# Exponentials of score tiles on VectorE: one pair with two private buffers, or two pairs that borrow their intermediates, in a new order

## The chip, the cores and the metric

The kernel runs on one core of one Trainium2 chip. The metric is the time of one execution in device microseconds; the kernel before took 1028.12 us (median of three runs, 1028.08 to 1029.24). TensorE does the matrix products, ScalarE (ACT in the profile) the exponentials and other activations, VectorE (DVE) most of the elementwise work, GpSimd (POOL) some small statistics and products, and SyncE (SP) issues most transfers.

## The reference

Two rounds of an attention layer and a mixer, over one sequence of 2048 positions with 448 channels. Attention has 16 heads of 28 channels. All weights are bfloat16.

```python
def _A_ref(x, wqkv, wo):                      # attention
    q, k, v = ...                             # x @ wqkv, split in 16 heads
    scores = jnp.einsum("bhqd,bhkd->bhqk", q, k) * (Dh ** -0.5)
    p = _softmax(scores, axis=-1)
    o = jnp.einsum("bhqk,bhkd->bhqd", p, v)
    return (...)(o, 0, 2, 1, 3).reshape(B, S, D) @ wo

def _B_ref(x, w1, w2, w3, w4):                # mixer
    h = _gelu(_layernorm(x, axis=-1) @ w1)
    ...                                       # four channel groups, shifted by -1, +1, -2, +2 positions
    hs = jnp.concatenate([g0, g1, g2, g3], axis=-1) @ w2
    x1 = x + hs
    h2 = _gelu(_layernorm(x1, axis=-1) @ w3) @ w4
    return x1 + h2

x = x + _A_ref(_layernorm(x, axis=-1), A_wqkv, A_wo)
x = x + _B_ref(_layernorm(x, axis=-1), B_w1, B_w2, B_w3, B_w4)
...                                           # the same two lines once more
```

What weighs most is the softmax: 2 layers x 16 heads x 2048 x 2048 exponentials, which is 2048 tiles of 128 x 512 scores.

## The kernel before

**A planner writes the order.** The program has no loops on the chip. While it is built, a planner (`Sched.run`) runs many small tasks, written as generators. Each yields operations with a planned duration and the tiles that they read and write, or asks for a resource (`acq`, `try`) or a signal. The planner hands the operations to five queues (TensorE, ScalarE, VectorE, GpSimd, SyncE), one by one, by its own planned clock and by priorities, and `Plan` then adds the semaphore waits. On the chip each engine works through its queue strictly in that order. So a number in a table of priorities or rates can move every instruction behind it.

**Scores.** Keys lie on the partitions. A score tile is 128 keys x 512 queries of one head. Four heads go together, so a block of 128 keys has four tiles. The queries are cut into chunks, the keys into ranges, and a *segment* is a chunk, a range and a group of four heads; there are 68 segments. `t_scores` takes the tiles in a fixed stream and puts them in turn into PSUM banks 0 to 2 (up to three tiles) and 3 to 5 (two tiles, now and then three). `t_exp` lets ScalarE turn each such unit into bfloat16 probabilities in `PT` (L1786, an instruction of 128x1024 or 128x1536). `t_pv` multiplies them with the values (L832), and sums in bank 7 over a segment. At the end of a segment VectorE copies bank 7 out (L1870, L1872).

**Tiles on VectorE.** Some tiles do not go to ScalarE. `t_scores` looks some key blocks ahead (`ahead_of`), and takes a tile there either into bank 2 in place of a unit's third tile (rates `R_RATE`, 6 to 8 blocks ahead) or into a free bank 5 or 6 (rates `D_RATE`, 5 to 7 blocks ahead). `d_first` (L1600) scales the tile out of PSUM into a 16-bit buffer `y`, and `d_chain` makes the exponential from the bits: a shift (L1627), a square (L1632), two multiply-and-adds (L1634, L1636), a product (L1638), a sum back into `y` (L1640), and per tile a last shift into a probability tile (L1646). Two tiles share a chain where two come soon enough after one another (a *pair*, 1024 wide); otherwise the chain is closed with one (512 wide). The width of the chain's operations is that of the pair, so a pair pays each of six instructions once.

**Buffers of a chain.** `y` and the first intermediate `q` are the two halves of `yd` (4 KB per partition, one pair at a time), or, in two stretches of the program in which some tiles of `vaug` are idle, four such tiles. The second intermediate `z` is a float buffer: one of the three `fb`, which the mixers' tanh steps (L2066 to L2069) and the softmax's normalization (L1893, L1897) use too, or in those stretches two tiles of `vaug`.

**The mixers** and projections run in between, on TensorE (L841), with their evacuations on VectorE and some elementwise steps on VectorE or GpSimd (table `XPAR`). Where TensorE would be idle in the plan, filler matmuls (L2299) are put in.

Of the kernel before, what the change touches and what calls it, by code (L numbers as in the profile page):

```python
# [552 lines left out]
R_RATE = {(0,): 0, (1,): 0.006, (2,): 0.016, (3,): 0.04, (4,): 0.006, (5,): 0.238, (6,): 0.059, (7,): 0.106, (8,): 0.06, (9,): 0.048, (10,): 0.024, (11,): 0.15, (12,): 0.066, (13,): 0.022, (14,): 0.018, (15,): 0.192, (16,): 0.233, (17,): 0.06, (18,): 0.115, (19,): 0, (20,): 0.093, (21,): 0.233, (22,): 0.355, (23,): 0.29, (24,): 0, (25,): 0.289, (26,): 0, (27,): 0.207, (28,): 0.183, (29,): 0.243, (30,): 0.071, (31,): 0.163, (32,): 0.241, (33,): 0.078}  # L553
# [22 lines left out]
XPAR = {'l0': 10, 'l1': 13, 'l2': 17, 'x0': 17, ('mg', 0, 0): 1, ('mg', 0, 1): 1, ('mg', 0, 2): 0, ('mg', 0, 3): 1, ('mg', 0, 4): 0, ('mg', 1, 0): 2, ('mg', 1, 1): 1, ('mg', 1, 2): 0, ('mg', 1, 3): 0, ('mg', 1, 4): 1, ('tw', 0, 0): 0, ('tw', 0, 3): 0, ('tw', 0, 7): 0, ('tw', 0, 11): 1, ('tw', 0, 13): 0, ('tw', 1, 0): 0, ('tw', 1, 3): 0, ('tw', 1, 7): 0, ('tw', 1, 11): 0, ('tw', 1, 13): 0, ('ek', 0, 0): 2, ('eo', 0, 0): 0, ('ek', 0, 1): 1, ('eo', 0, 1): 2, ('ek', 0, 2): 1, ('eo', 0, 2): 2, ('ek', 0, 3): 0, ('eo', 0, 3): 1, ('ek', 0, 4): 1, ('eo', 0, 4): 2, ('eq', 0, 0): 2, ('eq', 0, 1): 1, ('eq', 0, 2): 1, ('eq', 0, 3): 2, ('ez', 0, 0): 1, ('ez', 0, 3): 0, ('ez', 0, 7): 1, ('ez', 0, 11): 1, ('ez', 0, 13): 0, ('ez', 0, 4): 0, ('ez', 0, 8): 2, ('ez', 0, 12): 2, ('ez', 0, 14): 1, ('ex', 0, 0): 0, ('ex', 0, 1): 1, ('ex', 0, 2): 2, ('ex', 0, 3): 0, ('ex', 0, 4): 2, ('ex', 0, 5): 0, ('ex', 0, 6): 1, ('ex', 0, 7): 1, ('ex', 0, 8): 1, ('ex', 0, 9): 2, ('ex', 0, 10): 1, ('ex', 0, 11): 1, ('ex', 0, 12): 1, ('ex', 0, 13): 1, ('ex', 0, 14): 1, ('ex', 0, 15): 1, ('ek', 1, 0): 0, ('eo', 1, 0): 2, ('ek', 1, 1): 2, ('eo', 1, 1): 0, ('ek', 1, 2): 2, ('eo', 1, 2): 1, ('ek', 1, 3): 1, ('eo', 1, 3): 0, ('ek', 1, 4): 2, ('eo', 1, 4): 1, ('eq', 1, 0): 2, ('eq', 1, 1): 2, ('eq', 1, 2): 2, ('eq', 1, 3): 0, ('ez', 1, 0): 2, ('ez', 1, 3): 2, ('ez', 1, 7): 1, ('ez', 1, 11): 2, ('ez', 1, 13): 2, ('ez', 1, 4): 2, ('ez', 1, 8): 0, ('ez', 1, 12): 1, ('ez', 1, 14): 1, ('ex', 1, 0): 0, ('ex', 1, 1): 1, ('ex', 1, 2): 0, ('ex', 1, 3): 2, ('ex', 1, 4): 2, ('ex', 1, 5): 2, ('ex', 1, 6): 0, ('ex', 1, 7): 2, ('ex', 1, 8): 2, ('ex', 1, 9): 2, ('ex', 1, 10): 0, ('ex', 1, 11): 2, ('ex', 1, 12): 2, ('ex', 1, 13): 2, ('ex', 1, 14): 1, ('ex', 1, 15): 0, ('dt', 0): 0.742, ('dt', 1): 0.628, ('dt', 2): 0.754, ('dt', 3): 0.95, ('dt', 4): 0.834, ('dt', 5): 0.726, ('dt', 6): 0.327, ('dt', 7): 0.769, ('dt', 8): 0.514, ('dt', 9): 0.919, ('dt', 10): 0.95, ('dt', 11): 0.935, ('dt', 12): 0.755, ('dt', 13): 0.521, ('dt', 14): 0.877, ('dt', 15): 0.62, ('dt', 16): 0.663, ('dp', 0): 2.391, ('dp', 1): 2.567, ('dp', 2): 3.153, ('dp', 3): 2.433, ('dp', 4): 3.2, ('dp', 5): 1.698, ('dp', 6): 2.869, ('dp', 7): 1.898, ('dp', 8): 2.378, ('dp', 9): 2.988, ('dp', 10): 3.2, ('dp', 11): 3.081, ('dp', 12): 3.111, ('dp', 13): 3.2, ('dp', 14): 3.192, ('dp', 15): 3.2, ('dp', 16): 2.069, ('wt', 0): 0.173, ('wt', 1): 0.214, ('wt', 2): 0.438, ('wt', 3): 0.198, ('wt', 4): 0.329, ('wt', 5): 0.329, ('wt', 6): 0.17, ('wt', 7): 0.332, ('wt', 8): 0.414, ('wt', 9): 0.157, ('wt', 10): 0.38, ('wt', 11): 0.078, ('wt', 12): 0.009, ('wt', 13): 0.041, ('wt', 14): 0.163, ('wt', 15): 0.173, ('wt', 16): 0.372, ('ft', 0): 0.152, ('ft', 1): 0.146, ('ft', 2): 0.121, ('ft', 3): 0.157, ('ft', 4): 0.109, ('ft', 5): 0.073, ('ft', 6): 0.146, ('ft', 7): 0.029, ('ft', 8): 0.164, ('ft', 9): 0.024, ('ft', 10): 0.115, ('ft', 11): 0.041, ('ft', 12): 0.072, ('ft', 13): 0.183, ('ft', 14): 0.2, ('ft', 15): 0.146, ('ft', 16): 0.146, ('rp', 0): 1.476, ('rp', 1): 1.076, ('rp', 2): 0.876, ('rp', 3): 0.794, ('rp', 4): 0.794, ('rp', 5): 0.715, ('rp', 6): 0.645, ('rp', 7): 1.183, ('rp', 8): 0.857, ('rp', 9): 0.794, ('rp', 10): 0.842, ('rp', 11): 0.725, ('rp', 12): 0.707, ('rp', 13): 1.158, ('rp', 14): 0.794, ('rp', 15): 0.794, ('rp', 16): 0.621, ('pw', 0): 2, ('pw', 1): 2, ('pw', 2): 2, ('pw', 3): 2, ('pw', 4): 2, ('pw', 5): 4, ('pw', 6): 2, ('pw', 7): 3, ('pw', 8): 2, ('pw', 9): 4, ('pw', 10): 3, ('pw', 11): 1, ('pw', 12): 2, ('pw', 13): 3, ('pw', 14): 4, ('pw', 15): 2, ('pw', 16): 3}  # L576
# [25 lines left out]
def build_kernel(nc, A_x, A_wqkv, A_wo, B_x, B_w1, B_w2, B_w3, B_w4, out, n_layers=2):  # L602
# [79 lines left out]
    with st:  # L682
# [855 lines left out]
        def xtra(kind):  # L1538
            for ph, base in ((0, 16), (1, 9)):
                if ("xopen", ph) in SC.events and ("xshut", ph) not in SC.events:  # L1540
                    return {"y": ["ypv%d" % base], "f": ["fv%d" % (base + 4)], "pd": ["pv%d" % (base + 6)]}[kind]
            return []

        def t_extra(ph, base):
# [4 lines left out]
            for r in ("ypv%d" % base, "fv%d" % (base + 4), "pv%d" % (base + 6)):  # L1549
                yield ("acq", [r])  # L1550
# [14 lines left out]
        def ybuf(r):  # L1565
            if r[2] == "v":
                v, k = vbuf(r)
                w = vaug[:, int(r[3:]) + 2:int(r[3:]) + 4, :].rearrange("p a b -> p (a b)")
                return v, k, w, [("vaug", int(r[3:]) + 2), ("vaug", int(r[3:]) + 3)]
            return yd[:, 0, :], [("yd", 0)], yd[:, 1, :], [("yd", 1)]  # L1570
# [7 lines left out]
        def pbuf(r):  # L1578
            return ("vaug" if r[1] == "v" else "pd", int(r[2:]))

        PDS = ["pd%d" % i for i in range(NPD)]
        YS = ["yp0"]
        half = [None]

        def pair_of(ys, u):
# [817 lines left out]
```

## Time and profile before

| | |
|---|---|
| median of three runs | 1028.12 us (1028.08 to 1029.24) |
| the profiled execution | 1027.51 us, of it 1025.8 us span |
| TensorE busy | 973.4 us (95%), fillers included |
| ScalarE busy | 977.2 us (95%) |
| VectorE busy | 815.3 us (79%) |
| GpSimd busy | 194.8 us (19%) |
| granted TensorE clock | 1.00 |

Busy is the time in which an engine works on at least one instruction; instructions of one engine can overlap at their ends, so a group's mean duration times its count can be more than its busy time. The span leaves 1.7 us around it.

### The profile page before, as it was taken

Reading aid. Unit: us, or ns where it says so; the run is one execution under the profiler, and the core shown is the slowest. Engines: PE = TensorE matmul, PEld = TensorE weight load, DVE = VectorE, ACT = ScalarE, POOL = GpSimd, SP = SyncE. Lnnn points to the kernel's source line nnn. Section 1 sums busy time; section 2 is a strip of 40 time slices with the busy share of each in tenths; the row PEclk is TensorE's granted clock in tenths of the full one; section 3 lists DMA queues with packets and bytes.
Section 4 is the critical chain, followed back from the end, with each engine's and each line's share of the span. In section 5 each row is a group of like instructions: output and inputs, shape, how many; then the busy total and the mean of one; then the engine's idle time right before and its main releaser. Section 6 shows DMA issues by size and latency. Waiting matters only on the chain.

```text
span 1025.8 us, 36020 instructions
## 1 busy us (share of the span) xinstructions
PE 973.4 (95%) x16095; PEld 403.7 (39%) x16098; DVE 815.3 (79%) x1826; ACT 977.2 (95%) x900; POOL 194.8 (19%) x327
## 2 busy tenths in 40 slices
PE   8999999999999999999999999999999999999998
PEld 4333433433343334443434333333333333444465
DVE  8879999898757767887689779999898888787751
ACT  6899999999999999999999999999999999999933
POOL 4004012212222112220211000001431110431120
PEclk9999999999999999999999999999999999999999
DMA  4535324411113123220123124333311110231000
GB/s 126 130 73 167 64 54 106 146 31 46 25 22 96 24 67 69 52 44 14 43 61 82 42 71 132 110 75 101 84 28 34 41 45 13 55 61 18 12 21 25
DMA packets 98827, 64.41 MB, mean 63 GB/s; under 512 B 70832, under 2 KB 87552, under 8 KB 98672
## 3 DMA queue, kind: packets, MB, share of 16 engines
q1 hardware_dynamic: 94176, 53.11, 21.0%
q0 software_dynamic: 3376, 8.09, 2.9%
q8 instruction: 126, 2.06, 0.9%
q10 hardware_dynamic: 1120, 0.92, 0.3%
q14 instruction: 29, 0.24, 0.1%
HBM read 28.16 MB, written 16.76 MB: 44 GB/s over the span
## 4 chain that ended last, share of the span: by engine, by line
ACT 68%; PE 25%; DVE 6%; issue 1%; DMA 0%; ACTq 0%; DVEq 0%
ACT PT L1786 62%; PE ps L841 14%; PE ps L1488 6%; PE ps L832 4%; ACT h2T L2252 3%; ACT fb L2068 1%; ACT L1786 1%; DVE yd L1600 0%; DMA PT<-in_A_wqkv_dram 0%; ACT hT L2050 0%; PE ps L2299 0%; ACT L2252 0%; DVE vaug L1634 0%; DVE fb L1638 0%; ACT vaug L2252 0%
## 5 line engine op out<-in xcount | busy, mean ns | idle before, releaser
L1786 ACT ACTIVATE PT<-ps 128x1024 bf16<-128x1024 f32 (+1 forms) x793 | 882.0, 1304 | 6.0 <-PE ps L1488 4.9
L1488 PE MATMUL ps<-qT,kT 32*128 32x512 bf16 (+1 forms) x2560 | 310.1, 340 | 28.0 <-ACT PT L1786 20.7
L832 PE MATMUL ps<-PT,vaug 128*32 128x512 bf16 (+1 forms) x2411 | 244.1, 341 | 0.0
L1488 PEld LDWEIGHTS ps<-qT,kT 32*128 32x128 bf16 x2560 | 79.8, 91 | 298.8 <-ACT PT L1786 271.8
L841 PE MATMUL ps<-xT,w 128*32 128x512 bf16 (+4 forms) x2304 | 149.4, 336 | 0.0
L2299 PE MATMUL ps<-ident 128*32 128x256 bf16 x2900 | 132.6, 279 | 2.3 <-POOL ident L931 1.5
L832 PEld LDWEIGHTS ps<-PT,vaug 128*32 128x32 bf16 x2411 | 72.6, 94 | 90.8 <-issue 76.9
L841 PE MATMUL ps<-w,h2T 128*32 128x448 bf16 x1288 | 90.2, 355 | 3.7 <-ACT h2T L2252 3.7
L2299 PEld LDWEIGHTS ps<-ident 128*32 128x32 bf16 x2900 | 80.9, 98 | 28.8 <-issue 12.6
L1600 DVE TENSOR_SCALAR yd<-ps 128x512 int16<-128x512 f32 x84 | 57.7, 687 | 32.5 <-PE ps L1488 31.2
L841 PEld LDWEIGHTS ps<-xT,w 128*32 128x32 bf16 (+1 forms) x2304 | 61.1, 95 | 42.5 <-issue 22.5
L1897 POOL TENSOR_TENSOR otn<-ub,fb 128x512 bf16<-128x512 f32 (+1 forms) x27 | 32.5, 1205 | 220.2 <-DMA fb<-rscr 211.6
L2228 DVE CAST h2T<-ps 128x384 bf16<-128x384 f32 (+1 forms) x84 | 52.2, 621 | 20.4 <-PE ps L841 19.3
L841 PEld LDWEIGHTS ps<-w,h2T 128*32 128x32 bf16 x1288 | 33.9, 96 | 32.5 <-issue 12.8
L841 PE MATMUL ps<-kT,w 128*32 128x512 bf16 (+4 forms) x576 | 45.3, 350 | 0.9 <-DVE h2T L2228 0.5
L841 PE MATMUL ps<-xT,wq_pad 128*32 128x512 bf16 x512 | 45.0, 382 | 0.9 <-DVE kT L1227 0.8
L832 PE MATMUL ps<-PD,vaug 128*32 128x512 bf16 (+1 forms) x131 | 41.3, 347 | 0.8 <-DVE PD L1646 0.8
L841 PE MATMUL ps<-xT,wk_pad 128*32 128x512 bf16 (+2 forms) x512 | 38.9, 362 | 2.0 <-DVE kT L1227 1.4
L841 PE MATMUL ps<-wo_pad,otn 128*32 128x448 bf16 x512 | 37.4, 355 | 1.5 <-DVE x_res L1952 1.5
L841 PE MATMUL ps<-w,hT 112*32 112x448 bf16 x512 | 34.9, 355 | 4.1 <-ACT hT L2050 2.2
L2141 POOL TENSOR_SCALAR mst<-mv 128x1 f32<-128x1 f32 x32 | 8.8, 285 | 154.9 <-DVE mv L1052 154.9
L841 PE MATMUL ps<-wv,xT 128*32 128x448 bf16 x464 | 36.1, 356 | 1.2 <-DVE vaug L1334 0.4
(234 smaller groups left out, 1290.8 us busy)
## 6 DMA issues: line engine op xcount, KB each, us to landing
uscr<-ub SPq DMA_DIRECT2D x28, 256.0 KB
ub<-uscr SPq DMA_DIRECT2D x28, 256.0 KB, 2.8
fb<-rscr SPq DMA_DIRECT2D x96, 64.0 KB, 2.1
xnd<-xn SPq DMA_DIRECT2D x28, 128.0 KB, 2.5
x_res<-in_A_x_dram POOLq DMA_DIRECT2D x16, 224.0 KB, 2.7
xd<-x_res SPq DMA_DIRECT2D x16, 224.0 KB, 3.5
x_res<-xd SPq DMA_DIRECT2D x16, 224.0 KB, 4.2
out_dram<-obf SPq DMA_DIRECT2D x16, 112.0 KB
```

Of the source, the lines that this page charges most:

```text
L832: return lambda e: e.matmul(out=out, lhsT=lhsT, rhs=rhs, start=start, stop=stop, **kw)
L841: r.append(e.matmul(out=out[c:c + w, :], lhsT=lhsT[:, c:c + w], rhs=rhs, start=start, stop=stop, tile_position=(0, c)))
L1488: yield op("pe", (0.005 + NW * 0.00042) / nc_, lambda e, i=i, kc=kc, j=j, g=g, a=a, NW=NW, bank=bank: e.matmul(out=ps[:, bank, i * NW:(i + ...
L1600: yield op("dve", c_ps(512), lambda e: e.tensor_scalar(out=y.bitcast(I16)[:, 512 * h:512 * h + 512], in0=ps[:, bi(bank), :], scalar1=SCALE ...
L1786: yield op("act", 0.0635 + n * w * 0.000833, lambda e, bk=bk, s0=s0, n=n, w=w: e.activation(out=PT[:, s0:s0 + n, 0:w], in_=ps[:, bk[0]:bk[ ...
L1897: yield both(("eo", L, ch), 0.2 + NW * 0.00225, 0.07 + NW * 0.00104, lambda e: e.tensor_tensor(out=otn[:, g, 0:NW], in0=u, in1=rb[:, 0:NW] ...
L2068: yield op("act", c_act(NW), lambda e: e.activation(out=f, in_=f, func=ACT.Tanh, scale=8.0 * GK * (2.0 / math.pi) ** 0.5), reads=[fk], wri ...
L2141: yield op("pool", 0.2, lambda e: e.tensor_scalar(out=mst[:, t, V3E:V3E + 1], in0=mv[:, t, 1:2], scalar1=EPS, scalar2=None, op0=ALU.add), ...
L2228: ev = op("dve", c_ps(m * NW), lambda e, hr=hr, pv=pv: e.tensor_copy(out=hr, in_=pv), reads=[("ps", bi(b))], writes=hk, touch=[b])
L2252: yield op("act", c_act(len(fr_) * NW), lambda e, v=v: e.activation(out=v, in_=v, func=ACT.Gelu_apprx_tanh), reads=allk, writes=allk, tab= ...
L2299: return [e.matmul(out=ps[32 * c:32 * c + 32, bi(b), 0:256].rearrange("p (a n) -> p a n", n=128), lhsT=xn[:, 0, D:D + 32] if live else ide ...
```

## The change

The change has two parts. In the buffers, `y` and the first intermediate are parted: `yd` now holds two `y` of 2 KB each (`yp0`, `yp1`), so that two pairs can be under way, and the first intermediate becomes a second float buffer, which the chain asks for before its first shift and gives back at its end. The list of float buffers of the two idle stretches grows by the tiles that the first intermediate had there. In the order, five tables of the planner have other numbers: the rates at which tiles are taken (`R_RATE`, `D_RATE`), priorities (`RANK`), lead times (`Q_LEAD`) and `XPAR` (which engine takes some elementwise steps, thresholds and chain priorities).

```diff
-R_RATE = {(0,): 0, (1,): 0.006, (2,): 0.016, (3,): 0.04, (4,): 0.006, (5,): 0.238, (6,): 0.059, (7,): 0.106, (8,): 0.06, ...}
+R_RATE = {(0,): 0, (1,): 0.006, (2,): 0.016, (3,): 0.04, (4,): 0.006, (5,): 0.238, (6,): 0.037, (7,): 0, (8,): 0.169, ...}
...
@@ xtra
-                    return {"y": ["ypv%d" % base], "f": ["fv%d" % (base + 4)], "pd": ["pv%d" % (base + 6)]}[kind]
+                    return {"y": ["ypv%d" % base], "f": ["fv%d" % (base + 2), "fv%d" % (base + 4)], "pd": ["pv%d" % (base + 6)]}[kind]
@@ t_extra
-            for r in ("ypv%d" % base, "fv%d" % (base + 4), "pv%d" % (base + 6)):
+            for r in ("ypv%d" % base, "fv%d" % (base + 2), "fv%d" % (base + 4), "pv%d" % (base + 6)):
@@ ybuf
             if r[2] == "v":
-                v, k = vbuf(r)
-                w = vaug[:, int(r[3:]) + 2:int(r[3:]) + 4, :].rearrange("p a b -> p (a b)")
-                return v, k, w, [("vaug", int(r[3:]) + 2), ("vaug", int(r[3:]) + 3)]
-            return yd[:, 0, :], [("yd", 0)], yd[:, 1, :], [("yd", 1)]
+                return vbuf(r)
+            return yd[:, int(r[2:]), :], [("yd", int(r[2:]))]
@@
-        YS = ["yp0"]
+        YS = ["yp0", "yp1"]
@@ d_first
-            y, yk, _, _ = ybuf(pr["y"])
+            y, yk = ybuf(pr["y"])
@@ d_chain
-            y, yk, q, qk = ybuf(pr["y"])
+            y, yk = ybuf(pr["y"])
+            fq = yield ("acq", xtra("f") + FB, yk)
+            q_, qk = fbuf(fq)
+            q = q_.bitcast(BF16)
...
             yield ("rel", fr)
+            yield ("rel", fq)
```

More of the change, by code (lines that the diff above doesn't have):

```diff
@@ L552 @@
 DSEG = 1
-R_RATE = {(0,): 0, (1,): 0.006, (2,): 0.016, (3,): 0.04, (4,): 0.006, (5,): 0.238, (6,): 0.059, (7,): 0.106, (8,): 0.06, (9,): 0.048, (10,): 0.024, (11,): 0.15, (12,): 0.066, (13,): 0.022, (14,): 0.018, (15,): 0.192, (16,): 0.233, (17,): 0.06, (18,): 0.115, (19,): 0, (20,): 0.093, (21,): 0.233, (22,): 0.355, (23,): 0.29, (24,): 0, (25,): 0.289, (26,): 0, (27,): 0.207, (28,): 0.183, (29,): 0.243, (30,): 0.071, (31,): 0.163, (32,): 0.241, (33,): 0.078}
+R_RATE = {(0,): 0, (1,): 0.006, (2,): 0.016, (3,): 0.04, (4,): 0.006, (5,): 0.238, (6,): 0.037, (7,): 0, (8,): 0.169, (9,): 0.238, (10,): 0.048, (11,): 0.076, (12,): 0.066, (13,): 0.022, (14,): 0, (15,): 0.192, (16,): 0.156, (17,): 0.242, (18,): 0.053, (19,): 0.098, (20,): 0, (21,): 0.159, (22,): 0.357, (23,): 0.386, (24,): 0, (25,): 0.289, (26,): 0, (27,): 0.207, (28,): 0.255, (29,): 0.266, (30,): 0.098, (31,): 0, (32,): 0.241, (33,): 0.065}
 RLO = 6
@@ new lines @@
+Q_LEAD = {(0, 1): 7, (0, 2): 95, (0, 3): 64, (1, 0): 30, (1, 1): 99, (1, 2): 9, (1, 3): 66}
+D_RATE = {(0,): 0, (1,): 0, (2,): 0, (3,): 0.517, (4,): 0.133, (5,): 0.289, (6,): 0.447, (7,): 0.362, (8,): 0.092, (9,): 0.3, (10,): 0.129, (11,): 0.512, (12,): 0.005, (13,): 0.687, (14,): 0, (15,): 0.045, (16,): 0, (17,): 0.061, (18,): 0, (19,): 0.166, (20,): 0.403, (21,): 0, (22,): 0.477, (23,): 0, (24,): 0.39, (25,): 0, (26,): 0.293, (27,): 0.385, (28,): 0.064, (29,): 0.61, (30,): 0, (31,): 0.226, (32,): 0.513, (33,): 0.301}
```

6 lines of the change are left out of this document (2 added, 4 removed).

## The prediction

> **What bounds the kernel now.** I read the page first, its engine totals and the chain that ended last, then ScalarE's busy time by windows.
>
> ```profile
> PE 973.4 (95%) x16095; PEld 403.7 (39%) x16098; DVE 815.3 (79%) x1826; ACT 977.2 (95%) x900; POOL 194.8 (19%) x327
> ACT 68%; PE 25%; DVE 6%; issue 1%; DMA 0%; ACTq 0%; DVEq 0%
> ```
> ```profile
> core 0: us, PE busy (x) PEld busy (x) DVE busy (x) ACT busy (x) POOL busy (x), PEclk, DMA share, GB/s
> 0.00:25.00 25.00, 20.59 (x360) 10.88 (x361) 21.26 (x77) 17.05 (x24) 9.73 (x23) 1.00 0.42 129
> 25.00:100.00 75.00, 72.18 (x994) 24.82 (x1000) 61.31 (x147) 69.69 (x65) 14.72 (x21) 1.00 0.49 122
> sum 800.00, PE 761.23 PEld 304.00 DVE 657.32 ACT 798.14 POOL 146.56; mean PE 95.15 PEld 38.00 DVE 82.17 ACT 99.77 POOL 18.32
> ```
>
> Columns are a window's length and each engine's busy time with its count; the last row sums the eight windows of 100 us from 100 to 900. There ScalarE works 798.14 of 800 us, VectorE 657, 82%. TensorE's 95% is no bound of the same kind: the planner fills its gaps with filler matmuls. ScalarE has a hole of 8.0 us in the first 25 us, 5.3 in the next 75, almost none to 900, and after its last exponential it is not the bound: TensorE works off the last mixers. So a microsecond of exponentials taken off ScalarE is a microsecond of span, as long as TensorE and VectorE bring score tiles in time.
>
> What does an exponential cost? Instructions overlap at their ends, so I go by start to start.
>
> ```profile
> L1786 ACT ACTIVATE PT<-ps 128x1536 bf16<-128x1536 f32 x337 | 515.0, 1553 | 5.5 <-PE ps L1488 4.6
> L1786 ACT ACTIVATE PT<-ps 128x1024 bf16<-128x1024 f32 x456 | 483.6, 1120 | 0.5 <-PE ps L1488 0.3
> ```
> ```profile
> 361.08 57.80 ACT PT L1786 x52
> 952.27 1.34 ACT PT L1786
> 953.92 0.91 ACT PT L1786
> 972.16 1.28 ACT L2224
> ```
>
> The first fence groups instructions by form (count, busy, mean ns); the second is the chain in order of time (start, length, what). A step with three tiles takes 1.34, one with two 0.91 us, together 2.25 for five tiles; 52 unbroken steps give 57.80/26 = 2.22 per two. A tile is worth 0.45 us of ScalarE. The last row is the table load behind the last exponential, at 972.16: from there to the end of the span it is 53.6 us.
>
> **What the change removes.** The order that the changed program is built in has 334 instructions of 1536 and 453 of 1024: three fewer of each, 15 tiles, which VectorE takes (140 first operations L1600, 125 before). ScalarE's other work keeps its number of table loads (16), and one evacuation and one longer GELU swap. Removed: 3 x 2.25 = **6.8 us**.
>
> **What it adds on VectorE.** The words of the change promise pairs, but the order shows the reverse: chains of two fall from 43 to 31, chains of one rise from 39 to 78 (2 x 43 + 39 = 125; 2 x 31 + 78 = 140). Durations first, a chain of one that runs alone, then one whose operations alternate with others' (start, length):
>
> ```profile
> 660.42 0.29 DVE L1627 TENSOR_SCALAR vaug<-vaug 128x512 uint16<-128x512 uint16 x1
> 660.74 0.43 DVE L1632 TENSOR_TENSOR vaug<-vaug 128x512 bf16<-128x512 int16 x1
> 661.20 0.29 DVE L1634 TENSOR_SCALAR vaug<-vaug 128x512 bf16<-128x512 int16 x1
> 661.41 0.29 DVE L1636 TENSOR_SCALAR vaug<-vaug 128x512 bf16<-128x512 bf16 x1
> 661.73 0.43 DVE L1638 TENSOR_TENSOR vaug<-vaug 128x512 bf16<-128x512 bf16 x1
> 662.19 0.43 DVE L1640 TENSOR_TENSOR vaug<-vaug 128x512 int16<-128x512 int16 x1
> ...
> 674.93 0.28 DVE L1627 TENSOR_SCALAR vaug<-vaug 128x512 uint16<-128x512 uint16 x1
> 675.13 0.41 DVE L1640 TENSOR_TENSOR yd<-yd,fb 128x512 int16<-128x512 int16 x1
> 675.47 0.41 DVE L1632 TENSOR_TENSOR vaug<-vaug 128x512 bf16<-128x512 int16 x1
> 675.80 0.28 DVE L1646 TENSOR_SCALAR PD<-yd 128x512 uint16<-128x512 uint16 x1
> 676.01 0.28 DVE L1634 TENSOR_SCALAR vaug<-vaug 128x512 bf16<-128x512 int16 x1
> ```
> ```profile
> L1627 DVE TENSOR_SCALAR yd<-yd 128x1024 uint16<-128x1024 uint16 x29 | 12.3, 423 | 0.1
> L1632 DVE TENSOR_TENSOR fb<-yd 128x1024 bf16<-128x1024 int16 x26 | 19.8, 760 | 0.5
> L1634 DVE TENSOR_SCALAR yd<-yd 128x1024 bf16<-128x1024 int16 x29 | 13.2, 455 | 0.7
> L1636 DVE TENSOR_SCALAR fb<-fb 128x1024 bf16<-128x1024 bf16 x33 | 14.2, 432 | 0.0
> L1638 DVE TENSOR_TENSOR fb<-fb,yd 128x1024 bf16<-128x1024 bf16 x26 | 17.9, 688 | 0.4
> L1640 DVE TENSOR_TENSOR yd<-yd,fb 128x1024 int16<-128x1024 int16 x26 | 17.9, 690 | 0.6
> L1600 DVE TENSOR_SCALAR yd<-ps 128x512 int16<-128x512 f32 x84 | 57.7, 687 | 32.5 <-PE ps L1488 31.2
> L1646 DVE TENSOR_SCALAR PD<-yd 128x512 uint16<-128x512 uint16 x75 | 20.9, 301 | 1.1
> ```
>
> An operation followed by one that needs its result holds VectorE 0.03 longer than its duration (L1627 to L1632: 0.32 for 0.29); followed by another chain's operation, 0.08 less (0.20 for 0.28, 0.34 for 0.41, 0.33 for 0.41). The six durations add to 2.16 us for one tile, to 3.45 for a pair. Counting in the two orders which operation stands right before one that waits for it, a chain of one has 2.9 such places before and 1.8 after, a pair 2.7 and 2.2. So one costs 2.16 + 2.9 x 0.03 - 3.1 x 0.08 = 2.00 before and 1.88 after, a pair 3.27 and 3.21. Chains: 43 x 3.27 + 39 x 2.00 = 219 before, 31 x 3.21 + 78 x 1.88 = 246 after, +27. The 15 tiles add a first (0.69 - 0.08) and a last operation (0.30 - 0.08) each, +12. The mixers' steps that change sides between GpSimd and VectorE cancel to within 1 us. **VectorE +39 us, to about 855 (83%)**; without any overlap it would be 78 x 2.16 + 31 x 3.45 - 39 x 2.16 - 43 x 3.45 + 15 x 0.99 = +58.
>
> The Trainium skill ("VectorE: DVE Perf Modes", The DRAIN you can't avoid) says that the next operation does not start until the pipeline is empty and that a semaphore between two costs nothing, so only the number of operations counts; by that page the sum is the +58. Its next section lets an instruction that is not held start earlier, and the rows above agree with that: 0.20 against 0.32 after the same instruction.
>
> **Where VectorE has room for it.** 39 of its 210 idle us go, spread over everything; what counts is the fullest stretch, first layer, first and second chunk with the later keys, between the 12th and the 20th copy of bank 7:
>
> ```profile
> 113.50:246.60 133.10, 125.07 (x2003) 50.95 (x1998) 121.38 (x248) 132.80 (x122) 26.30 (x37) 1.00 0.32 80
> 250.00:374.00 124.00, 119.41 (x1792) 44.28 (x1786) 85.71 (x176) 123.63 (x105) 27.93 (x45) 1.00 0.18 43
> 150.00:175.00 25.00, 23.02 (x371) 9.32 (x363) 23.90 (x53) 24.90 (x24) 5.88 (x7) 1.00 0.30 79
> ```
>
> In 133.1 us VectorE works 121.4. The new order puts 35 first operations there (27 before), 9 pairs (12) and 14 chains of one (5): 9 x 3.21 + 14 x 1.88 - 12 x 3.27 - 5 x 2.00 = +6.0, and 8 x 0.83 = +6.6, so 134.0 us of VectorE work. ScalarE's falls by 8 x 0.45 to 129.2. Here VectorE is asked for more than ScalarE, by 4.8 us. That need not stop ScalarE: the tiles are taken 5 to 8 key blocks ahead, at 4 x 0.45 = 1.8 us each, so a chain may end 9 us late or more before TensorE waits for its tile, and the stretch behind has 38 us of VectorE idle to catch up. I take 2 us of holes in ScalarE, between 0 and the bound worked out under the rivals.
>
> **The wait that is added.** A chain asks for its first float buffer before its first shift. Behind that request, in the plan, stand only other askers of a float buffer: the tanh steps and the normalization's broadcasts. The normalization's product on GpSimd is off the path (GpSimd is 19% busy), so I cost it at nothing; with that cover gone it would be an output projection one transfer later, at the end of a chunk, and in the last chunk no transfer of that kind is used.
>
> **The tail.** After the last exponential the new order still has two more tiles of the 1-layer mixer (five L2137 there, three before) and 32 more of the w2 matmuls, but as many fewer of others: 1193 matmuls against 1197. What moves is one block of 32 matmuls from ahead of the last GELU to behind it,
>
> ```profile
> 976.96 1.05 PE L841 MATMUL ps<-xT,w 128*32 128x256 bf16 x32
> ```
>
> 1.05 us: **+1.0**.
>
> **Sum.** Against the profiled execution (1027.51 us, of it 1025.8 span): 1027.5 - 6.8 + 2.0 + 1.0 = 1023.7. That execution is 0.6 under the median, so **1024.3 us**. A measurement of this kernel can tell about 0.2%, 2.1 us, from no change.
>
> **The rivals.**
>
> *VectorE takes over as the bound (slower).* Place: 113.5 to 246.6. In its fullest 25 us VectorE reached 23.90, 0.956. If it can't do better and its arrears are not carried on, the stretch lasts 134.0/0.956 = 140.2 us, 7.1 more than now, and only the other 7 tiles gain, 3.2: 1028.1 + 7.1 - 3.2 + 1.0 = 1033.0. It decides when the arrears at 246 pass what the look-ahead allows, about 9 us; 140.2 - 129.2 = 11 would. For it: VectorE is asked for over 100% of the stretch. Against: at 0.956 ScalarE still had 24.90 of 25. 24%.
>
> *A longer tail (no change).* The two mixer tiles left for the end go through product, statistics, GpSimd, norm, a transfer and three matmul groups; if TensorE can't fill this with other work, VectorE's three steps alone,
>
> ```profile
> L2137 DVE SCALAR_TENSOR_TENSOR x1b<-x_res,mst,ps 128x448 f32<-128x448 f32 x32 | 21.3, 670 | 19.9 <-PE ps L841 18.4 <-DVE x_res L2152 0.9 <-issue 0.5
> L1051 DVE BATCH_NORM_STATS2 st<-x1b 128x6 f32<-128x448 f32 x32 | 19.6, 618 | 0.4
> L1071 DVE TENSOR_SCALAR xn<-x1b,mv,mst 128x448 bf16<-128x448 f32 x32 | 17.4, 546 | 1.3 <-POOL mst L2143 1.3
> ```
>
> are 1.83 us a tile, 3.7 for two: 1028.0. For it: that chain is serial. Against: the order puts 112 + 224 + 168 matmuls between. 11%.
>
> *Full cost per operation (slower).* If the added operations overlap with nothing, the stretch gets 9 x 2.16 - 3 x 3.45 + 8 x 0.99 = +17.0, 138.4/0.956 = 144.8, and 1028.1 + 11.7 - 3.2 + 1.0 = 1037.6. The rows at 674.93 speak against it. 2%. (This is what the page's DRAIN rule would make of the change.)
>
> That the change does less than it says is so for the pairs, but not for the 15 tiles: they are counted in the built order.
>
> **How the numbers follow.** Forecast 63%, rivals 24, 11 and 2. The forecast's own range is 1019.5 to 1027: without holes and tail 1021.3, and up to 1.8 better if the new order also closes some of the 13.3 us of holes in the first 100 us; upward, half of the rival's loss. The range reaches to the first rival: 1019.5 to 1033. Faster by over 0.2% 0.62, within 0.13, slower 0.25.
>
> **What would show it.** Right: 787 exponentials, ScalarE busy near 970, its busy share from 100 to 900 still above 99.5%, VectorE near 855. Wrong: idle time before L1786 or before the score matmuls L1488 that ends on L1600 or on a chain's L1646, in a stretch of VectorE above 0.96; a span between last exponential and end of more than 56 us; or VectorE busy above 870, which would be the price without overlap.

## The result, and the profile after

The changed kernel took 1041.78 us (median of four runs, 1040.32 to 1044.49) against 1028.15 us of the kernel before beside it: a ratio of 1.0133, with a 95% interval of 1.0108 to 1.0158. It is slower by 13.6 us, where the prediction said 3.8 us faster. The profiled execution took 1042.96 us, of it 1041.0 us span.

The page of the changed kernel, busy time and the chain that ended last, and the one group of ScalarE's exponentials:

```profile
PE 978.7 (94%) x16102; PEld 407.8 (39%) x16102; DVE 848.2 (81%) x2016; ACT 970.9 (93%) x893; POOL 197.1 (19%) x330
ACT 63%; PE 32%; DVE 2%; DMA 2%; issue 0%; ACTq 0%; DVEq 0%; SPq 0%
L1788 ACT ACTIVATE PT<-ps 128x1024 bf16<-128x1024 f32 (+1 forms) x787 | 874.2, 1301 | 25.3 <-PE ps L1488 20.3
```

The work changed as forecast: 787 exponentials, ScalarE 6.3 us less busy (977.2 to 970.9), VectorE 33 us more (815.3 to 848.2). But the idle time ahead of the exponentials is 25.3 us, and the chain has 2% of DMA that it did not have. Where the idle time lies is read from windows, first of the kernel before, then of the changed one (length, then busy time of TensorE, its weight loads, VectorE, ScalarE and GpSimd, the granted clock, DMA share, GB/s):

```profile
75.00:125.00 50.00, 47.40 (x730) 18.04 (x723) 46.16 (x141) 49.57 (x48) 12.45 (x17) 1.00 0.46 118
125.00:525.00 400.00, 381.18 (x6338) 155.11 (x6342) 311.09 (x648) 399.27 (x353) 86.34 (x145) 1.00 0.23 57
525.00:600.00 75.00, 72.74 (x1123) 28.85 (x1115) 62.09 (x120) 74.80 (x71) 6.18 (x13) 1.00 0.19 55
```
```profile
75.00:125.00 50.00, 37.70 (x478) 12.86 (x482) 31.93 (x111) 34.96 (x33) 14.27 (x22) 0.83 0.73 189
125.00:525.00 400.00, 382.20 (x6393) 158.68 (x6393) 341.37 (x763) 398.29 (x350) 68.35 (x126) 1.00 0.21 45
525.00:600.00 75.00, 72.78 (x1133) 28.81 (x1130) 66.23 (x130) 70.35 (x73) 21.50 (x27) 1.00 0.29 63
```

ScalarE (the fifth number) lost 14.6 us between 75 and 125 (49.57 to 34.96), where the granted clock is 0.83 and the DMA engines move 189 GB/s instead of 118, and 4.45 us between 525 and 600. From 125 to 525 it lost 1.0, and 0.7 in the first 75 us. From the last exponential's table load to the end it is 54.4 us instead of 53.6. Less work and more idle time together, -6.3 + 14.6 + 4.45 + 1.0 + 0.8 + 0.7 = +15.2 us, are the difference of the two spans.

What ended the wait between 75 and 125: the waits there, the step of the chain, and the instruction that waited longest on TensorE.

```profile
ACT PT L1788 <- PE ps L1488: 15.0, 6, 11.7
PE ps L841 <- DMA xT<-xnd: 11.0, 1, 11.0
```
```profile
87.41 18.50 DMA xT<-xnd
105.96 1.47 PE ps L841 x12
```
```profile
105.96 1.47 PE L841 MATMUL ps<-xT,wk_pad 128*32 128x512 bf16 x12 [10.99 <-DMA xT<-xnd]
```

ScalarE waits for scores (L1488); these stand behind a key projection (L841, `wk_pad`) in TensorE's order; and that waits for `xT`, a transposed load (a DMA_TRANSPOSE on SP's queue) of normalized rows. It started at 87.41 and landed 18.5 us later. What else was under way then is on GpSimd's queue, first of the changed kernel, then of the kernel before (start, time to issue, what, and in brackets the idle time before it and its end):

```profile
84.68 0.78 POOL L881 DMA_DIRECT2D w<-in_B_w_dram  x1
85.43 0.57 POOL L882 DMA_DIRECT2D w<-in_B_w_dram  x1
85.97 1.14 POOL L883 DMA_DIRECT2D w<-in_B_w_dram  x1
87.07 2.20 POOL L1933 DMA_DIRECT2D x_res<-in_A_x_dram  x4
196.80 0.47 POOL L1557 MEMSET vaug<- 128x448 bf16 x1 [107.53 <-PE ps L832]
```
```profile
138.37 1.28 POOL L1897 TENSOR_TENSOR otn<-ub,fb 128x512 bf16<-128x512 f32 x1 [50.84 <-DMA fb<-rscr]
...
174.63 1.51 POOL L1897 TENSOR_TENSOR otn<-ub,fb 128x512 bf16<-128x512 f32 x1 [10.73 <-DMA fb<-rscr]
176.09 0.92 POOL L881 DMA_DIRECT2D w<-in_B_w_dram  x1
177.01 0.55 POOL L882 DMA_DIRECT2D w<-in_B_w_dram  x1
177.55 1.12 POOL L883 DMA_DIRECT2D w<-in_B_w_dram  x1
```

L881 to L883 load the mixers' large weights, w3 (1344 and 224 KB) and w4 (1568 KB). They have no wait of their own: they start when GpSimd's queue reaches them. Before, four normalization products (L1897) stood ahead of them, each waiting for a transfer, and held them until 176. In the changed kernel nothing that waits is left ahead of them; they start at 84.7 instead of 176.1, some 3 us before the transposed load. Four loads of 224 KB each behind them (L1933, `x_res`) come along: they start at 87.1, and in the kernel before, at 151.8, behind two of the products. Nobody needs any of these so early.

Two numbers of the new table `XPAR` do this. `('eo', 0, 0)`, from 0 to 1, gives the four products of the first chunk to VectorE. `l2`, from 17 to 14, lets the task that loads the weights ask for w3 and w4 at the start of segment 14 instead of 17, which in the planned order lies ahead of these products. Each is enough by itself in the order that the planner writes (not run on the chip): with only `l2` back at 17 no instruction that waits stands ahead of the loads, and with only the products back on GpSimd the loads stand ahead of all four.

### The profile page after: what moved, and what is told of

Read it like the earlier page. It is cut to its first block, busy times and chain, and to the rows that moved or that the text cites. A ratio compares the mean times of both kernels' runs of the same rounds, so it can differ in the third digit from the quotient of the medians.

```text
span 1041.0 us, 36214 instructions
## 1 busy us (share of the span) xinstructions
PE 978.7 (94%) x16102; PEld 407.8 (39%) x16102; DVE 848.2 (81%) x2016; ACT 970.9 (93%) x893; POOL 197.1 (19%) x330
## 4 chain that ended last, share of the span: by engine, by line
ACT 63%; PE 32%; DVE 2%; DMA 2%; issue 0%; ACTq 0%; DVEq 0%; SPq 0%
ACT PT L1788 56%; PE ps L841 17%; PE ps L1488 8%; PE ps L832 5%; ACT h2T L2254 3%; DMA xT<-xnd 2%; PE ps L2301 2%; ACT fb L2070 1%; ACT hT L2052 1%; ACT L1788 1%; ACT L2052 0%; DMA PT<-in_A_wqkv_dram 0%; ACT vaug L2254 0%; ACT kT L2254 0%; ACT L2254 0%
## 5 line engine op out<-in xcount | busy, mean ns | idle before, releaser
L1788 ACT ACTIVATE PT<-ps 128x1024 bf16<-128x1024 f32 (+1 forms) x787 | 874.2, 1301 | 25.3 <-PE ps L1488 20.3
L1488 PE MATMUL ps<-qT,kT 32*128 32x512 bf16 (+1 forms) x2560 | 310.0, 341 | 22.8 <-ACT PT L1788 16.6
L832 PE MATMUL ps<-PT,vaug 128*32 128x512 bf16 (+1 forms) x2393 | 245.6, 342 | 1.3 <-DVE ub L1874 0.8
L1488 PEld LDWEIGHTS ps<-qT,kT 32*128 32x128 bf16 x2560 | 79.5, 91 | 293.7 <-ACT PT L1788 260.7
L841 PE MATMUL ps<-xT,w 128*32 128x512 bf16 (+4 forms) x2592 | 176.8, 344 | 3.7 <-DVE h2T L2230 1.7
L2301 PE MATMUL ps<-ident 128*32 128x256 bf16 x2288 | 111.0, 280 | 2.0 <-POOL ident L931 1.5
L832 PEld LDWEIGHTS ps<-PT,vaug 128*32 128x32 bf16 x2393 | 72.1, 94 | 94.0 <-issue 76.6
L1598 DVE TENSOR_SCALAR yd<-ps 128x512 int16<-128x512 f32 x115 | 78.9, 687 | 22.9 <-PE ps L1488 21.5
L841 PE MATMUL ps<-w,h2T 128*32 128x448 bf16 x1288 | 89.8, 355 | 2.7 <-ACT h2T L2254 2.7
L841 PEld LDWEIGHTS ps<-xT,w 128*32 128x32 bf16 (+1 forms) x2592 | 67.8, 95 | 56.8 <-issue 29.6
L2301 PEld LDWEIGHTS ps<-ident 128*32 128x32 bf16 x2288 | 66.9, 98 | 23.0 <-issue 7.6
L841 PE MATMUL ps<-xT,wk_pad 128*32 128x512 bf16 (+1 forms) x512 | 42.2, 388 | 12.6 <-DMA xT<-xnd 11.0
L2301 PE MATMUL ps<-ident,xn 128*32 128x256 bf16 x1116 | 51.9, 274 | 0.0
L841 PEld LDWEIGHTS ps<-w,h2T 128*32 128x32 bf16 x1288 | 35.2, 96 | 30.9 <-issue 13.1
L832 PE MATMUL ps<-PD,vaug 128*32 128x512 bf16 (+1 forms) x150 | 43.9, 348 | 0.0
L841 PE MATMUL ps<-wv,xT 128*32 128x448 bf16 x480 | 38.2, 363 | 2.5 <-DVE vaug L1334 1.5
L841 PE MATMUL ps<-wo_pad,otn 128*32 128x448 bf16 x512 | 37.8, 356 | 2.1 <-DVE x_res L1954 1.2
L841 PE MATMUL ps<-xT,wq_pad 128*32 128x512 bf16 x448 | 37.9, 382 | 1.1 <-DVE kT L1227 0.8
L1227 DVE TENSOR_SCALAR kT<-ps,cols 128x512 bf16<-128x512 f32 (+2 forms) x35 | 23.7, 682 | 17.6 <-PE ps L841 17.6
L841 PE MATMUL ps<-w,hT 112*32 112x448 bf16 x512 | 34.1, 354 | 3.9 <-ACT hT L2052 3.0
```

Of the source, the lines that this page charges most:

```text
L832: return lambda e: e.matmul(out=out, lhsT=lhsT, rhs=rhs, start=start, stop=stop, **kw)
L841: r.append(e.matmul(out=out[c:c + w, :], lhsT=lhsT[:, c:c + w], rhs=rhs, start=start, stop=stop, tile_position=(0, c)))
L1227: evacs = [("dve", c_ps2(NW), lambda e: e.tensor_scalar(out=dst, in0=ps[:, bi(b), 0:NW], scalar1=MK, scalar2=None, op0=ALU.add)), ("act", ...
L1488: yield op("pe", (0.005 + NW * 0.00042) / nc_, lambda e, i=i, kc=kc, j=j, g=g, a=a, NW=NW, bank=bank: e.matmul(out=ps[:, bank, i * NW:(i + ...
L1598: yield op("dve", c_ps(512), lambda e: e.tensor_scalar(out=y.bitcast(I16)[:, 512 * h:512 * h + 512], in0=ps[:, bi(bank), :], scalar1=SCALE ...
L1788: yield op("act", 0.0635 + n * w * 0.000833, lambda e, bk=bk, s0=s0, n=n, w=w: e.activation(out=PT[:, s0:s0 + n, 0:w], in_=ps[:, bk[0]:bk[ ...
```

## The experiments

The kernel before was timed again beside each group; its median there was 1027.6 to 1028.4 us. In the expectations, theory A says that these loads, in flight when the transposed load starts, cost the 14.6 us; its rivals are named there. Theory B of this first group says that VectorE is behind with its work and the hole is only where it shows. The runs on the rest of the gain use the letter B for another theory, given there. Except in `buffers_only` and `own_plan`, the edits are made behind the planner: the order of all instructions that they don't name stays.

### The loads

**`after_hold`**: the changed kernel, with one wait given to the first of the three loads, on the TensorE product that stands last before it in the written order (135 us).

```diff
         est = SC.run()
+        PO = P.ops["pool"]
+        LD = [o for o in PO if o.dma and "w3" in o.fn.__code__.co_freevars][0]
+        LD.deps["pe"] = [o for o in P.ops["pe"] if o.pos < LD.pos][-1]
```

> The changed kernel with one added wait: the first of the three loads of w3 and w4 (2.98 MB, GpSimd's queue) waits for the last matmul that the plan has ahead of it, the start of segment 14; no instruction changes its place. Theory A (the loads leave at 85 us instead of some 135, and hold up the transposed load of normalized x for keys and values, 18.5 us, and with it TensorE and ScalarE): the hole of 14.6 us in ScalarE between 75 and 125 us goes, that transposed load lands within 5 us, and the time falls to 1027 (1025 to 1029). Theory B (VectorE is in arrears and the hole is only where it shows): within 3 us of the changed kernel's 1041.8.

1027.26 us against 1027.88, ratio 0.9994 (0.9985 to 1.0004), span 1026.2. Its windows:

```profile
75.00:125.00 50.00, 49.20 (x719) 18.39 (x719) 44.19 (x147) 47.81 (x46) 8.80 (x14) 0.97 0.53 128
125.00:525.00 400.00, 383.21 (x6428) 159.65 (x6426) 341.71 (x747) 399.08 (x352) 75.79 (x136) 1.00 0.25 57
525.00:600.00 75.00, 72.65 (x1078) 26.67 (x1071) 67.42 (x145) 70.34 (x72) 19.57 (x25) 1.00 0.16 46
```

One wait, on the first of the three loads, gives back 14.5 us. The two others and the four `x_res` loads stand behind it in the queue and wait with it (they start at 135.6 to 138.1). With that the change is worth nothing measurable: between 75 and 125 ScalarE still has 1.8 us less than before, and the 4.5 us between 525 and 600 are still lost.

**`before_early`** and **`before_collide`**: the kernel before, with the three loads moved up in GpSimd's queue, behind the w2 load (they start at 87.3, and the nearest transposed load was at 68.6), or with a wait that lets them start right before a transposed load.

```diff
...
+        for q in (PO, P.all):
+            for o in LD:
+                q.remove(o)
+            q[q.index(W2[0]) + 1:q.index(W2[0]) + 1] = LD
```
```diff
...
+        GATE = P.ops["pe"][396]
...
+        LD[0].deps["pe"] = GATE
```

> The kernel before with the three loads of w3 and w4 moved up in GpSimd's queue to right behind the load of w2, so that they leave at 87 us as in the changed kernel; all other instructions keep their places. In this kernel the transposed loads run at 68.8 and 115.2 us, and none between. Theory A (a collision with one transposed load): within 3 us of before, 1027 to 1031. Theory C (3 MB that early slow everything that moves, whatever stands beside it): 1035 or more.

1028.75 us, ratio 1.0005 (0.9994 to 1.0017). Early by itself costs nothing measurable.

> The kernel before with the same three loads placed so that they leave at 67 us, tied to a matmul there, right ahead of the transposed load that starts at 68.8 us; all other instructions keep their places, and VectorE's work is that of before. Theory A: that transposed load takes over 10 us instead of 2 to 3, TensorE waits for it, and the time rises by 8 to 16 us, to 1036 to 1044. Theory B (VectorE's arrears cause the loss): within 3 us of before.

1050.89 us, ratio 1.0205 (1.0181 to 1.0228): more than expected. The two w3 loads start at 70.74 and 71.76, the transposed load at 72.03, w4 at 72.31, and the chain shows

```profile
72.03 26.99 DMA xT<-xnd
```

27 us for a load that no TensorE instruction waited for in the kernel before. In its later half the other bulk loads (`x_res`, `wo_pad`, w1, w2, from 83.9 on) were issued as well. So the harm needs only the kernel before and a neighbour in time; nothing of the new buffers or rates takes part in it.

**`hold_w4`**: the changed kernel with the last of the three loads (w4) held, and with it the `x_res` loads behind it in the queue (they start at 144.9); w3 still starts ahead of the transposed load, at 85.1.

```diff
+        LD = [o for o in PO if o.dma and "w3" not in o.fn.__code__.co_freevars and "w4" in o.fn.__code__.co_freevars][0]
+        LD.deps["pe"] = [o for o in P.ops["pe"] if o.pos < LD.pos][-1]
```

> The changed kernel with only the w4 load held (1.6 MB), the two w3 loads (1.6 MB) still start at 84.7 us, ahead of the transposed load: half of what collides. Theory A with the cost by bytes in flight: the transposed load takes 8 to 12 us instead of 18.5, ScalarE's hole from 100 to 125 falls from 12.4 to 2 to 6 us, the time is 1029 to 1036. Rival (any bulk load ahead of a transposed load costs the whole stall, whatever its size): transposed load 16 us or more, time 1039 to 1043. Rival (only the last load, issued right before it, matters): transposed load under 5 us, time 1026 to 1029.

1036.12 us (one run), just above the range that the cost by bytes gave; its chain has

```profile
87.89 12.09 DMA xT<-xnd
```

12.09 us with w3 (1.6 MB) beside it, 18.50 with w3, w4 and `x_res` (4.1 MB). ScalarE's longest hole is 5.25 us instead of 11.66. More bytes in flight make a longer stall (two points), and the rivals (any bulk load costs the whole stall; only the last one counts) fall. What share of the difference is w4's and what `x_res`'s, no run separates. The DMA view of the changed kernel shows the order in which they were served: from 88 to 98 the bulk queue moved nearly all, from 98 to 106 both did (queue, packets, MB, share of 16 engines).

```profile
q0 software_dynamic: 550, 2.80, 97.4%
q1 hardware_dynamic: 320, 0.08, 5.0%
```
```profile
q0 software_dynamic: 750, 1.58, 73.1%
q1 hardware_dynamic: 1914, 0.74, 55.1%
```

The transposed load's queue is q1. In its first ten us all of q1 got 0.08 MB through, but 320 packets against 550 of q0: 0.25 KB and 5.1 KB each. The Trainium skill ("DMA: Bandwidth & Descriptors", Queues, rings and completion order) says that each DMA engine takes turns between the queues that have work, a whole packet at a time. The rows agree, if the profile's packets are the page's, which no run here shows: by packets the two are not far apart, by bytes the queue with small packets gets 3%, as long as the large ones last.

**`buffers_only`**: the new buffers with the old five tables, planned anew.

> The buffers of the change (two y of 2 KB, both intermediates in float buffers) with the five tables of before; the planner writes another order from it. In it the loads of w3 and w4 stand behind four products on GpSimd that wait for the normalization, so they leave late. Theory A: no hole of over 5 us in ScalarE before 200 us; time by ScalarE's work, within 8 us of before, 1022 to 1036. Theory B: VectorE busier than before and holes spread behind it, above 1036.

1062.71 us, ratio 1.0332 (1.0318 to 1.0346). The time misses theory A's range and lies in theory B's, and VectorE is busier (838 us against 815). But VectorE is not full where ScalarE waits: it works 18.2 and 21.8 of 25 us in the two stretches with the largest holes, 11.2 us from 225 to 250 and 16.8 from 550 to 575. The loads start at 176.5 and nothing waits for a transposed load. TensorE has 17,286 products. The kernel before has 16,098 (by its weight loads), and all 1,188 more are fillers, so the planner knew of holes when it wrote the order. The run does not part the buffers from the order: old tables in a planner with other buffers give another order, and that order is bad. The parts of this change can't be had one by one that way; except in `own_plan`, single instructions were moved in a fixed order from here on.

### The rest of the expected gain

In the changed kernel the hole at 566 to 570 ends on a group of TensorE's products, one of them with a VectorE tile (L832, at 569.68). In TensorE's order it stands right where that tile's chain ends (start, length, what):

```profile
549.36 0.29 DVE L1628 TENSOR_SCALAR fb<-yd 128x512 uint16<-128x512 uint16 x1
...
565.70 0.68 DVE L2071 SCALAR_TENSOR_TENSOR vaug<-fb,vaug 128x512 bf16<-128x512 f32 x1
566.42 0.42 DVE L1633 TENSOR_TENSOR fb<-fb 128x512 bf16<-128x512 int16 x1
...
569.34 0.28 DVE L1648 TENSOR_SCALAR PD<-yd 128x512 uint16<-128x512 uint16 x1
```
```profile
570.06 3.28 ACT L1788 ACTIVATE PT<-ps 128x1536 bf16<-128x1536 f32 x3 [3.97 <-PE ps L832]
```

Between the chain's first and second operation lie 17.06 us. It holds one float buffer and waits for the second, until a mixer's tanh step (L2071) gives one back. In the kernel before the longest such wait is 9.61 us. TensorE itself idles only 0.73 us in the hole: it works on projections and fillers, which the order has there. Theory B of the next two runs: this wait is the hole.

**`hold_own`**: as `after_hold`, and this one chain uses the free half of its own `y` tile as second buffer; its six remaining operations move up behind the first, on VectorE alone.

```diff
...
+    _cells(rest[0])["z"].cell_contents = yd[:, yk[1], :].bitcast(BF16)[:, 512:1024]
...
+    for o in rest:
+        at += 1
+        while seq[at].eng != "dve":
+            at += 1
+        at += 1
+        seq.insert(at, o)
+    _replay(P, seq)
```

> The changed kernel with the held loads, and one chain more moved: the chain of one whose first shift stands at 534.40 us and whose multiplication L1633 comes only at 551.47, 17.1 us later, since its second float buffer is with a tanh step. Here that chain takes the free half of its own y tile as its second buffer, and its remaining six operations stand right behind the first shift, each behind one other VectorE instruction. Nothing else moves. Theory B (the hole of 4.0 us in ScalarE at 551 is the chain that holds one float buffer and waits for the second: the tile comes late, TensorE's product with it stands in front of the score matmuls): that hole goes, ScalarE busy in 550 to 575 rises from 20.44 to over 24, the span falls by 3.5 to 4.6 from 1026.2 to about 1022, the time to 1022.5 to 1024, 0.4 to 0.5% under the kernel before. Rival (VectorE is simply full there, 23.2 of 25 us, and something else comes late in the chain's place): the hole stays above 2 us and the time stays within 1.5 us of 1027.3.

1028.02 us against 1028.38, ratio 0.9998 (0.9989 to 1.0008): B's number is missed, and the rival's came (a hole of 3.08 us stays). The chain is done 15 us earlier, and ScalarE still has 23.90 and 21.33 of 25 us from 525 to 575. TensorE shows why: its order still has the product with that tile where the late tile had put it, behind two projections and a run of fillers.

```profile
552.93 0.74 PE L841 MATMUL ps<-w,h2T 128*32 128x448 bf16 x12
553.50 0.61 PE L2301 MATMUL ps<-ident,xn 128*32 128x256 bf16 x16
553.95 0.83 PE L841 MATMUL ps<-xT,w 128*32 128x384 bf16 x16
554.60 0.40 PE L832 MATMUL ps<-PT,vaug 128*32 128x512 bf16 x2
554.62 0.38 PE L832 MATMUL ps<-PD,vaug 128*32 128x512 bf16 x1
```

**`own_plan`**: the same buffer for the same chain, but given to the planner, which then writes everything behind 528 us anew.

```diff
...
+            own = blks[0] == (35, 6, 2)
+            fr = None if own else (yield ("acq", xtra("f") + FB, qk))
+            z_, fk = (y, yk) if own else fbuf(fr)
...
```

> The changed kernel with the held loads, planned anew with one difference: the chain of the tile that waited 17.1 us for its second float buffer takes the free half of its own y tile instead, so the planner never lets it wait, and everything behind it on every engine is ordered anew (up to there the order is the same). Moving that chain's VectorE operations alone did not close the hole, since TensorE still followed an order written for a late tile. Theory B': the hole at 545 to 555 is written into TensorE's order by that wait; here ScalarE works 24.5 us or more in each 25 us from 525 to 575 (23.9 and 21.3, or 24.9 and 20.4, in the runs so far). Rival: VectorE has no room there (23.2 of 25 us); then the hole stays within 25 us of its place, at 3 us or more. Behind 580 the order is another one that no table was set for, with holes of its own, so its whole time, 1040 to 1055, says nothing on either theory.

```profile
525.00:550.00 25.00, 24.76 (x343) 8.74 (x340) 21.86 (x46) 24.90 (x26) 12.26 (x16) 1.00 0.17 30
550.00:575.00 25.00, 23.93 (x359) 9.12 (x351) 22.91 (x46) 25.00 (x26) 4.48 (x5) 1.00 0.28 76
575.00:600.00 25.00, 23.87 (x365) 8.87 (x365) 22.42 (x52) 20.66 (x20) 3.17 (x5) 1.00 0.29 73
```
```profile
600.73 0.20 ACT L1433 ACTIVATE fct<-dbc 128x4 f32<-128x4 f32 x1 [5.08 <-DVE dbc L1447]
```

In the two stretches that the expectation names, ScalarE works 24.90 and 25.00 us, with VectorE at 22.9 of 25: at that place VectorE has room, and the hole goes when the planner never lets this chain wait. But a hole of 5.08 us, on other instructions, now ends at 600.7, and from 525 to 600 ScalarE works 70.56 us, no more than the 70.34 of `after_hold`. So the run bears theory B out at the hole's place, though everything else behind 528 is in a new order too. It does not show that the 4.45 us can be had back, for work put off there may come due behind it. (It is one run; its whole time, 1048.37 us, comes from holes behind 575, as expected.) The wait is real on the chip and was already a fact of the order: it could have been seen before any run.

**`hold_all`** and **`hold_cast`**: what is left between 75 and 125. `hold_all` is `hold_own` with a wait for the first bulk loads too (x_res, wo_pad, w1, w2), until the transposed load has landed. `hold_cast` is `hold_all` without the moved chain of `hold_own`, and with two other operations moved on VectorE: in `after_hold` TensorE waited there for an evacuation (L1334) behind a chain's sum (L1641) that took 1.15 us,

```profile
73.34 1.15 DVE L1641 TENSOR_TENSOR yd<-yd,vaug 128x512 int16<-128x512 int16 x1
74.40 0.61 DVE L1334 CAST vaug<-ps 128x448 bf16<-128x448 f32 x1
```
```profile
75.07 0.37 PE L841 MATMUL ps<-wv,xT 128*32 128x448 bf16 x4 [1.55 <-DVE vaug L1334]
```

and `hold_cast` puts that chain's product and sum (L1639, L1641) behind the evacuation and the statistics that follow it. The last two lines of the diff are the wait that both kernels have.

```diff
...
+        PR = [o for o in DV if o.fn.__code__.co_firstlineno in (1639, 1641)][:2]
+        AT = [o for o in DV if o.fn.__code__.co_firstlineno == 1405][-1]
...
+        k = seq.index(AT) + 1
+        seq[k:k] = PR
+        _replay(P, seq)
...
+        LX = [o for o in P.ops["pool"] if o.dma][0]
+        LX.deps["pe"] = [o for o in P.ops["pe"] if o.pos > X4.pos and any(_split(a)[0] == ("xT", 1) for a in o.rw[0])][0]
```

> As the kernel with the moved chain, and the first of GpSimd's bulk loads (x_res, then wo_pad, w1, w2 behind it) also gets a wait, on the first product with the rows that the transposed load at 86.5 us brings. In the run with only the late loads held, that transposed load, beside the loads issued from 76.9 on, took 3.71 us and ScalarE had 2.1 us of holes from 75 to 81, before it; against 0.3 in the kernel before. Theory A (bulk loads beside a transposed load are what costs): the transposed load falls to 2 to 2.5 us; that saves at most the 1.5 us, and only if a score tile waits for it. The holes at 75 to 81 lie before that transposed load, so they stay, 2.1 us. Rival (the early holes come from the bulk loads too, which start at 76.9): they shrink below 1 us, and the span is 1 to 2 us shorter than that of the kernel with the moved chain alone. Time by A: within 1 us of that kernel.

1028.77 us against 1028.38, ratio 1.000 (0.999 to 1.001). The transposed load is issued in 1.92 us instead of 3.71, and ScalarE keeps 22.91 of 25 us from 75 to 100 (22.94 in `after_hold`): as A expected, those holes are not the loads' doing.

> The changed kernel with the late loads held and the first bulk loads held too, and two operations moved on VectorE: the product L1639 and the sum L1641 of a chain at 72.9 us, which stood ahead of the evacuation L1334 that TensorE waits for, go behind the statistics that follow it. In the runs so far the sum took 1.15 us there (0.42 is usual), beside GpSimd's four products of 70.9 to 75.3, TensorE waited 1.5 us for the evacuation, and ScalarE had 2.1 us of holes from 75 to 81. Theory D (those holes are this chain's two operations, ahead of the evacuation and slowed by GpSimd): TensorE's wait falls under 0.5 us, ScalarE's holes from 75 to 81 fall to 0.3 to 0.9 us, and the time is 1.2 to 1.8 us under that of the kernel without the move, 1026 us, within what these rounds can just tell. Rival (TensorE itself is short there: the changed order puts more projection work ahead of the scores): the wait goes and the holes stay above 1.5 us.

1025.01 us against 1028.14, ratio 0.997 (0.9959 to 0.9981); span 1022.8.

```profile
75.00:125.00 50.00, 48.88 (x740) 18.79 (x737) 45.55 (x142) 49.87 (x49) 7.98 (x13) 1.00 0.48 129
525.00:600.00 75.00, 72.66 (x1071) 26.66 (x1068) 67.45 (x144) 70.34 (x71) 18.27 (x23) 1.00 0.16 46
```

TensorE's wait fell from 1.55 to 0.28 us,

```profile
73.25 0.37 PE L841 MATMUL ps<-wv,xT 128*32 128x448 bf16 x4 [0.28 <-DVE vaug L1334]
```

and ScalarE works 49.87 of 50 us from 75 to 125, against 47.8 to 48.4 in the four runs with held loads and without the move. Theory D holds; the time fell a little more than it said. The two moved operations now take 0.42 us each, and no run separates their place from the sum's length. This version beats both kernels, by 3.1 us the one before and by 16.8 the changed one, and still has the 4.66 us of holes from 525 to 600.

## Why the prediction was wrong

**The step that failed** is the cost of what changes sides. "What it adds on VectorE" says: "The mixers' steps that change sides between GpSimd and VectorE cancel to within 1 us." "The wait that is added" says of the normalization's product on GpSimd that it is "off the path (GpSimd is 19% busy), so I cost it at nothing". Both count the time of the steps themselves and take it as the whole cost. What a step had held in GpSimd's queue was not asked, nor where `l2` puts the loads, and the sum has no term for a transfer. In the changed kernel the loads had lost what held them, a transposed load beside them took 18.5 us, and ScalarE lost 14.6 us. Neither the sum nor a rival names that, so the whole range missed. The facts were there: the trace of before has the products' waits, of up to 51 us, ahead of L881 to L883, and the built order of the changed program has the loads without them. How much a transposed load suffers could not be read from it, since no L1198 load had started beside these loads.

**The gain of 6.8 us** measured 6.3 of ScalarE's busy time, from 787 exponentials as counted. Right.

**VectorE +39, to 855** measured +33, to 848. Right in kind and a little high. "Above 870" did not come.

**Holes of 2 us, from the fullest stretch, 113.5 to 246.6** was wrong in place and mis-sized. From 150 to 250 ScalarE has no hole with VectorE busy at 22.80 to 24.53 of each 25 us, so the rival that VectorE takes over falls at that place. But 4.45 us came between 525 and 600, and, with the loads held, 1.8 between 75 and 125. In both a VectorE chain stood in the way by its place in an order and not by VectorE's total; for the second `hold_cast` shows it, for the first `own_plan` bears it out at the hole's place, and what would win the 4.45 us back stays open. The step that missed the first is "The wait that is added": it looked for who stands behind the request for the first float buffer, and not at a chain that holds one and waits for the second.

**The tail, +1.0**, measured +0.8. Right.

So with the loads held the sum would have been 1027.5 - 6.3 + 4.45 + 1.8 + 0.8 = 1028.2; the profiled execution of `after_hold` took 1028.18 and the median 1027.26: the forecast of a gain falls even without the loads, since the holes take what the exponentials give.

## What to carry to other kernels

When an instruction moves off an in-order queue, list what stands behind it there: a transfer without a wait of its own starts as soon as the queue reaches it, however late the plan meant it, and what held it may have been an instruction that had nothing to do with it. Give a bulk load that is not urgent an explicit wait, and keep it away from small loads that a compute engine waits for. And where one task takes a second shared buffer while it holds a first, look in the written order for the gap between the two. Here moving the late operations alone was not enough, because TensorE's order was written for the late time.

## What the runs showed that was not expected

A transposed load took 12.1 us from start to landing with the w3 loads (1.6 MB) beside it, 18.5 with w3, w4 and `x_res` (4.1 MB), and 27.0 when w3 was issued 1.3 and 0.3 us before it, w4 0.3 us after it and 2.1 MB more from 12 us after it. In `after_hold`, with 2.1 MB issued 3.4 to 9.6 us before it, no engine waited for it. With TensorE starved, the granted clock of 75 to 100 and 100 to 125 was 0.89 and 0.77; in `hold_cast` it was 1.00 in both. And a small sum on VectorE (128x512, 16 bits) took 1.15 us while GpSimd worked on products (in `after_hold` until 75.3), and 0.42 in `hold_cast`, 0.7 us after GpSimd's last product. The Trainium skill ("GPSIMD Engine Reference", in the table of its specifications) says that GpSimd shares its SBUF interfaces with VectorE and that VectorE instructions with two SBUF inputs contend for them, which this sum is; the two durations agree with it. The chain's product (L1639) just ahead, two inputs as well, started at 72.89, a moment before GpSimd's products of 72.91 to 75.38, and took its usual 0.41.
